# An adaLN transformer block with its gradients on one core: the preparation rewritten, and V, later Q, norms and modulation rows made inside the first attention chunk

## The chip, the cores and the metric

The kernel runs on one core of a Trainium2 chip. The metric is the device time of one execution in microseconds, from the first to the last instruction. Times of the kernel before are those of seven runs, and one more execution was taken with the hardware profiler. The core's engines are called PE (TensorE, matmuls; PEld is its weight load), DVE (VectorE), ACT (ScalarE), POOL (GpSimd) and SP (SyncE, which here only issues DMAs).

## What is computed

One transformer block with adaptive layer norm, and the gradients of all its parameters for a given output gradient. Sequence 2048, width 512, 32 heads of 16, hidden width 1792, all in bf16:

```
mod = (silu(c) @ w_mod).reshape(1, 6, 1, 512)        # sa, ca, ga, sb, cb, gb
h = layernorm(x) * (1 + ca) + sa
q, k, v = heads(h @ wqkv)
p = softmax(q @ k^T / 4)
x = x + ga * ((p @ v) @ wo)
h = layernorm(x) * (1 + cb) + sb
x = x + gb * (relu(h @ w1 + b1)**2 @ w2 + b2)
# results: x, and d/d(x, wqkv, wo, w1, b1, w2, b2, c, w_mod) of sum(x * grad_out)
```

## The kernel before

All work is on tiles of 128 partitions. The 2048 tokens are 16 tiles `t`, in four chunks of four tiles. There are four stages.

*Preparation* (L145 to L294, in pools of its own that are given back at its end). Loads, then for each chunk `g`: `layernorm(g)` takes statistics (bn_stats and bn_aggr on DVE), the reciprocal root by four Newton steps on DVE (`rsqrt_cols`), normalises on ACT, multiplies by `ca` and adds `sa` on DVE (rows spread over partitions, from `mod_rows(1)` and `mod_rows(0)`), and turns the result with DMA transposes into `h1T`. `qkv(g)` makes K, Q and V by tokens, twelve matmuls a tile, copies them out of PSUM, and turns K and Q with DMA transposes into `qkT`; all goes to DRAM (`qkT_st`, `v_st`, `k_st`, `q_st`), V also into `vaug` in SBUF, with a column of ones per head. `norms(g)` squares `qkT`, sums over each head with a selecting matmul, takes the greatest norm of the keys (`kmx`) and the root of those of the queries (`qn`). At the end `m_st` gets, for each head and query, minus the product of the two: the bound that is taken off the scores by an added row in `qt_sb`. Then come the modulation rows 2 to 5, their columns (`pcol`) and `b1col`. In preparation a scheduler orders the engines' work.

*Attention forward* (from L901). From here the written order is the order on each engine. A unit `u` is a chunk of 512 queries, a group of four heads and a tile of 128 keys: 4 x 8 x 16 = 512 units. `fscore(u)` makes four score matmuls of 32 rows into two PSUM pairs (`psST`, three buffers) and two Exp on ACT, each 128x1024, into `ET` (four buffers). `fpv(u - 2)` adds the products with `vaug` into `oacc`. Every 16 units `fload` loads the next group's K into `kts`, and Q and the row of `m_st` into `qts`, nine DMAs; `oacc` goes out through `ostage`, four DMAs to `rrows` and one DMA transpose to `O_un`. Beside this, each unit does at most one piece of other work through `step`: from the second chunk on, that is the dense half of the block and its gradients for the chunk before. All that other work shares one PSUM buffer, `pm`, from `mm()`. In the first chunk there is no such work; in its place SP runs `later_stage(u // 4)` and `turn_weights(u // 4)`, which turn V and the weights by DMA transposes for later stages. `later(lag, ...)` puts a call `lag` units further on; a DMA that `sp` issues waits in SP's queue, in order, for whatever it needs.

*The last chunk's dense half*, then *attention backward* (from L1457; 1300 us, half the span) and *the last products* follow. The change does not touch them, except that they read what the preparation stored: `k_st`, `q_st`, `vT_st`, `mean1`, `rstd1`, `rows_st`, `modcol`, `b1col`.

The unit loop before, as it bears on the change:

```
for u in range(NF + 2):
    unit[0] = u
    run_due()
    if u < NF:
        if funits[u][2] == 4 and u + TT < NF:
            fload(*funits[u + TT][0:2])
        fscore(u)
    if 2 <= u:
        fpv(u - 2)
    if u % 4 == 2 and u // 4 < 32:
        later_stage(u // 4)
    if u % 4 == 0 and u // 4 < 16:
        turn_weights(u // 4)
    if u < NF - 4:
        step(u)
```

Of the kernel before, what the change touches and what calls it, by code (L numbers as in the profile page):

```python
# [15 lines left out]
ALU = mybir.AluOpType  # L16
# [18 lines left out]
def kernel(  # L35
# [109 lines left out]
    with ExitStack() as ph:  # L145
        big = ph.enter_context(tc.tile_pool(name="prepB", bufs=1))
        wk = ph.enter_context(tc.tile_pool(name="prepW", bufs=2))
        psA = ph.enter_context(tc.tile_pool(name="psA", bufs=2, space=bass.MemoryType.PSUM))
        c_col = wk.tile([P, DC], BF, name="c_col", bufs=1)
        SP.dma_start(out=c_col[:], in_=c.rearrange("o (ic p) -> p (o ic)", p=P))  # L150
        x0_tok = big.tile([P, TT, D], BF, name="x0_tok")
        SP.dma_start(out=x0_tok[:, 0:4, :], in_=x_dram[:, 0:4, :])
        wmod_v = w_mod.rearrange("(ic p) j -> p ic j", p=P)
        wmod_nat = big.tile([P, DC, 6 * D], BF, name="wmod_nat")
        SP.dma_start(out=wmod_nat[:, :, 0:2 * D], in_=wmod_v[:, :, 0:2 * D])
        wqkv_nat = big.tile([P, DC, 3 * D], BF, name="wqkv_nat")
        SP.dma_start(out=wqkv_nat[:], in_=A_wqkv.rearrange("(ic p) j -> p ic j", p=P))
        for g in range(1, QC):
            SP.dma_start(out=x0_tok[:, 4 * g:4 * g + 4, :], in_=x_dram[:, 4 * g:4 * g + 4, :])
        SP.dma_start(out=wmod_nat[:, :, 2 * D:], in_=wmod_v[:, :, 2 * D:])  # L160
        b1bf = wk.tile([P, FC], BF, name="b1bf", bufs=1)
        SP.dma_start(out=b1bf[:], in_=B_b1.rearrange("(fc p) -> p fc", p=P))
        cbf = wk.tile([1, D], BF, name="cbf", bufs=1)
        SP.dma_start(out=cbf[:], in_=c[0:1, :])

        sig_col = wk.tile([P, DC], F32, name="sig_col", bufs=1)
        ACT.activation(sig_col[:], c_col[:], AF.Sigmoid)
        siluc_col = wk.tile([P, DC], BF, name="siluc_col", bufs=1)
        DVE.tensor_tensor(siluc_col[:], c_col[:], sig_col[:], ALU.mult)
        sbcT = big.tile([P, DC, P], BF, name="sbcT")  # L170
        DVE.tensor_copy(sbcT[:], siluc_col[:].unsqueeze(2).to_broadcast([P, DC, P]))
        crows = wk.tile([1, 3, D], F32, name="crows", bufs=1)
        ACT.activation(crows[:, 1, :], cbf[:], AF.Sigmoid)
        POOL.tensor_copy(crows[:, 0, :], cbf[:])
        POOL.tensor_tensor(crows[:, 2, :], crows[:, 0, :], crows[:, 1, :], ALU.mult)
        SP.dma_start(out=rows_st[6:9, :].unsqueeze(0), in_=crows[0:1, :, :])

        def mod_rows(j):
            pm = psA.tile([P, 512], F32, name="pm", tag="pm")
            for ic in range(DC):  # L180
                PE.matmul(pm[:], sbcT[:, ic, :], wmod_nat[:, ic, j * 512:(j + 1) * 512],
                          start=(ic == 0), stop=(ic == DC - 1))
            if j in (1, 4):
                DVE.tensor_scalar(modbc[:, j, :], pm[:], 1.0, None, ALU.add)
            else:
                ACT.activation(modbc[:, j, :], pm[:], AF.Identity)


        sel = big.tile([P, 4, H], BF, name="sel")
        POOL.memset(sel[:], 0.0)  # L190
        sel8 = wk.tile([P, 8], F32, name="sel8", bufs=1)
        DVE.tensor_reduce(sel8[:], identb.rearrange("p (i d) -> p i d", d=DH), AX.X, ALU.add)
        for b in range(4):
            POOL.tensor_copy(sel[:, b, 8 * b:8 * b + 8], sel8[:])
        POOL.memset(vaug[:, :, H, :], 1.0)
        POOL.memset(vaug[:, :, :, DH:DH + 1], 1.0)
        for i in range(2):
            POOL.memset(kts[i][:], 1.0)
            POOL.memset(qts[i][:], 0.0)

        h1T = big.tile([P, TT, DC, P], BF, name="h1T")
        qkT = big.tile([P, 8, n], BF, name="qkT")
        qn = big.tile([H, n], F32, name="qn")
        kmx = wk.tile([H, QC], F32, name="kmx", bufs=1)

        def layernorm(g):
            mv4 = wk.tile([P, 4, 2], F32, name="mv4p", tag="mv4p")
            for ti in range(4):
                st6 = wk.tile([P, 6], F32, name="st6p", tag="st6p")
                DVE.bn_stats(st6[:], x0_tok[:, 4 * g + ti, :])  # L210
                DVE.bn_aggr(mv4[:, ti, :], st6[:])
            gs = slice(4 * g, 4 * g + 4)
            rsqrt_cols(wk, rstd1[:, gs], mv4[:, :, 1], 4)
            DVE.tensor_copy(mean1[:, gs], mv4[:, :, 0])
            nb4 = wk.tile([P, 4], F32, name="nb4p", tag="nb4p")
            DVE.scalar_tensor_tensor(out=nb4[:], in0=mv4[:, :, 0], scalar=-1.0, in1=rstd1[:, gs], op0=ALU.mult, op1=ALU.mult)
            h1_g = wk.tile([P, 4, D], BF, name="h1_g", tag="h1_g")
            for ti in range(4):
                t = 4 * g + ti
                xn1 = wk.tile([P, D], BF, name="xn1", tag="xn1")  # L220
                ACT.activation(xn1[:], x0_tok[:, t, :], AF.Identity, bias=nb4[:, ti:ti + 1], scale=rstd1[:, t:t + 1])
                DVE.tensor_tensor(h1_g[:, ti, :], xn1[:], ca1_bc, ALU.mult)
                DVE.tensor_tensor(h1_g[:, ti, :], h1_g[:, ti, :], sa_bc, ALU.add)
                if ti % 2 == 1:
                    SP.dma_start(out=h1T[:, t - 1:t + 1].rearrange("p t i q -> p (t i) q"),
                                 in_=h1_g[:, ti - 1:ti + 1, :].rearrange("p t d -> p (t d)"), transpose=True)

        def qkv(g):
            qkv_g = wk.tile([P, 4, 3 * D], BF, name="qkv_g", tag="qkv_g")
            for ti in range(4):  # L230
                t = 4 * g + ti
                for which in (1, 0, 2):
                    pq = psA.tile([P, D], F32, name="pqkv", tag="pqkv", bufs=3)
                    for ic in range(DC):
                        PE.matmul(pq[:], h1T[:, t, ic, :], wqkv_nat[:, ic, which * D:(which + 1) * D],
                                  start=(ic == 0), stop=(ic == DC - 1))
                    dst = qkv_g[:, ti, which * D:(which + 1) * D]
                    if which == 0:
                        DVE.tensor_copy(dst, pq[:])
                    else:  # L240
                        ACT.activation(dst, pq[:], AF.Identity)
                SP.dma_start(out=qkT[:, :, t * P:(t + 1) * P], in_=qkv_g[:, ti, 0:2 * D], transpose=True)
# [27 lines left out]
        for g in range(QC):  # L270
            if g + 1 < QC:
                layernorm(g + 1)
# [1507 lines left out]
```

## Time and profile before

| what | us |
|---|---|
| median of 7 runs | 2637.76 (2627.47 to 2644.49) |
| the profiled execution | 2638.39 |
| its span, first to last instruction | 2636.6 |
| first score matmul (L705) / first Exp (L707) | 104.2 / 106.2 |
| dense half of the last chunk | about 1108 to 1220 |
| attention backward | about 1220 to 2520 |

The mean granted clock of TensorE was 0.883 of full speed over the span. The page gives busy time of each engine, the span in 40 equal slices, and the costliest groups of instructions, each with what ended the idle time before it. The chain of waits follows the work that ended last back to what released it. A busy share is an average over stages with different limits, so it is read by stages.

### The profile page before, as it was taken

How to read it: one execution, taken by the hardware profiler on the slowest of the kernel's cores; microseconds unless marked ns; L12 is line 12 of the kernel's file. 1: busy time of each engine (PE TensorE's matmuls, PEld its weight loads, DVE VectorE, ACT ScalarE, POOL GpSimd, SP SyncE). 2: the span in 40 equal slices, each digit the busy share in tenths (PEclk: the TensorE clock that was granted, in tenths of full speed). 3: DMA queues.
4: the chain of work that ended last, by engine and by line, in shares of the span. 5: the costliest groups of instructions: out<-in, count | busy, mean ns of one | idle time of the engine just before them, and what ended most of it. 6: DMA issues, size and time to landing. Idle time of an engine off the chain costs nothing.

```text
span 2636.6 us, 48844 instructions
## 1 busy us (share of the span) xinstructions
PE 2376.2 (90%) x18110; PEld 747.9 (28%) x18183; DVE 1748.5 (66%) x2234; ACT 2321.3 (88%) x3594; POOL 362.1 (14%) x369
## 2 busy tenths in 40 slices
PE   6699989988988889899999999999999999999999
PEld 2211112322322232352222222222222222222243
DVE  7101134434443544568999999998999998989962
ACT  4599999998999899855999999999999999999952
POOL 2100010211242223201110101101011010110100
PEclk8655559986999799998999999998999999999999
DMA  8853366335855775798999999999999999999982
GB/s 241 197 149 123 99 154 139 83 109 157 134 98 100 155 135 118 173 257 190 198 200 199 203 197 202 195 199 195 193 198 195 194 198 195 195 193 205 193 244 82
DMA packets 1254800, 453.74 MB, mean 172 GB/s; under 512 B 1130127, under 2 KB 1225363, under 8 KB 1254306
## 3 DMA queue, kind: packets, MB, share of 16 engines
q1 hardware_dynamic: 1226642, 415.77, 80.0%
q0 software_dynamic: 10944, 16.78, 4.5%
q10 hardware_dynamic: 16976, 18.07, 2.5%
q8 instruction: 143, 2.34, 0.4%
q14 instruction: 95, 0.78, 0.1%
HBM read 97.08 MB, written 73.95 MB: 65 GB/s over the span
## 4 chain that ended last, share of the span: by engine, by line
PE 43%; ACT 37%; issue 6%; DVE 5%; DMA 3%; SPq 1%; ACTq 0%; POOL 0%; DVEq 0%; POOLq 0%
ACT E_u L1346 20%; ACT ET L707 13%; PE dqacc L1418 6%; PE psS_A L1340 4%; PE psST L705 4%; PE accVK L1391 3%; ACT dsT L1489 3%; PE psS_C L1340 2%; PE pm L380 2%; PE psS_B L1340 2%; PE oacc L721 2%; PE pm L545 2%; PE accVK L1400 2%; PE pdh L1604 2%; PE pwq L1638 2%
## 5 line engine op out<-in xcount | busy, mean ns | idle before, releaser
L1360 DVE TENSOR_TENSOR dS_u<-psD_u,E_u 128x1024 bf16<-128x1024 f32 x1024 | 1186.4, 1215 | 106.5 <-PE psS_B L1340 55.1
L707 ACT ACTIVATE ET<-psST 128x1024 bf16<-128x1024 f32 x1024 | 945.0, 1296 | 43.7 <-PE psST L705 43.2
L1346 ACT ACTIVATE E_u<-psS_A 128x512 bf16<-128x512 f32 x768 | 509.6, 664 | 24.0 <-PE psD_u L1358 8.4
L1346 ACT ACTIVATE E_u<-psS_B 128x512 bf16<-128x512 f32 x768 | 504.8, 657 | 6.2 <-PE ptT L1381 1.2
L705 PE MATMUL psST<-qt_sb,kt_sb 32*128 32x512 bf16 x2048 | 412.8, 468 | 62.8 <-ACT ET L707 27.3
L1358 PE MATMUL psD_u<-iv,ido 32*128 32x512 bf16 x2048 | 425.7, 401 | 1.9 <-DVE dS_u L1360 1.7
L1346 ACT ACTIVATE E_u<-psS_C 128x512 bf16<-128x512 f32 x512 | 335.1, 654 | 1.5 <-PE accVK L1400 0.8
L1340 PE MATMUL psS_B<-ik,iq 32*128 32x512 bf16 x768 | 308.3, 401 | 11.8 <-ACT E_u L1346 4.4
L1340 PE MATMUL psS_A<-ik,iq 32*128 32x512 bf16 x768 | 306.7, 399 | 13.0 <-ACT E_u L1346 2.0
L721 PE MATMUL oacc<-ET,vaug 128*32 128x512 bf16 x2048 | 248.9, 476 | 5.9 <-DVE ostage L725 5.9
L1391 PE MATMUL accVK<-dS_u,qz 128*32 128x512 bf16 x2048 | 226.3, 412 | 0.5 <-DVE dS_u L1360 0.4
L1340 PE MATMUL psS_C<-ik,iq 32*128 32x512 bf16 x512 | 195.4, 382 | 32.9 <-ACT dsT L1489 28.8
L1340 PEld LDWEIGHTS <-iq 32*128 32x128 bf16 x2048 | 129.3, 92 | 309.0 <-issue 293.5
L1400 PE MATMUL accVK<-E_u,dOs_tok 128*16 128x512 bf16 x2048 | 208.3, 397 | 0.0
L705 PEld LDWEIGHTS <-kt_sb 32*128 32x128 bf16 x2048 | 90.2, 94 | 399.9 <-issue 388.7
L1436 POOL TENSOR_TENSOR dQacc<-dQacc,dqtmp 128x512 f32<-128x512 f32 x64 | 81.3, 1270 | 873.6 <-ACT dqtmp L1431 873.6
L1418 PE MATMUL dqacc<-dsT,KS_tok 128*32 128x512 bf16 x2048 | 180.7, 462 | 12.9 <-DMA dsT<-dS_u 3.5
L725 DVE COPY ostage<-oacc 128x512 f32<-128x512 f32 x32 | 22.0, 688 | 229.8 <-PE oacc L721 182.1
L1489 ACT ACTIVATE dsT<-ptT 128x1024 bf16<-128x1024 bf16 x128 | 148.5, 1160 | 3.3 <-PE ptT L1381 3.0
L398 DVE COPY part<-pm 128x512 f32<-128x512 f32 (+2 forms) x103 | 63.4, 616 | 132.5 <-PE pm L380 124.8
L1358 PEld LDWEIGHTS <-ido 32*128 32x128 bf16 x2048 | 107.3, 92 | 108.4 <-issue 103.9
L1391 PEld LDWEIGHTS <-qz 128*32 128x32 bf16 x2048 | 60.8, 98 | 241.0 <-issue 228.3
(342 smaller groups left out, 2255.8 us busy)
## 6 DMA issues: line engine op xcount, KB each, us to landing
p_st<-part POOLq DMA_DIRECT2D x36, 256.0 KB, 5.6
kt_sb<-qkT_st SPq DMA_DIRECT2D x128, 64.0 KB
wA<-in_B_w_dram SPq DMA_DIRECT2D x28, 256.0 KB
dsT<-dS_u SPq DMA_TRANSPOSE x448
wB<-w1T_st SPq DMA_DIRECT2D x21, 256.0 KB
wA<-w2T_st SPq DMA_DIRECT2D x21, 256.0 KB
wB<-in_B_w_dram SPq DMA_DIRECT2D x21, 256.0 KB
p_st<-part POOLq DMA_DIRECT2D x25, 192.0 KB, 4.1
```

The costliest lines, as they stand in the source:

```text
L705: PE.matmul(ps[:, hi, :], kt_sb[r:r + 32, kt * P:(kt + 1) * P], qt_sb[r:r + 32, :], start=True, stop=True, tile_position=(r, 0))
L707: ACT.activation(ET[:, 2 * pair:2 * pair + 2, :], ps[:], AF.Exp, scale=SCALE)
L721: PE.matmul(oacc[32 * hq:32 * hq + 32, :], lhsT, ET[:, hq, :], start=(kt == 0), stop=(kt == TT - 1), tile_position=(0, 32 * hq), skip_grou ...
L1340: PE.matmul(psS[:], st["q"][r:r + 32, qt * P:(qt + 1) * P], st["k"][r:r + 32, kc * 512:kc * 512 + 512], start=True, stop=True, tile_positi ...
L1346: ACT.activation(bst[u][0][:, hq, :], sst.pop((u, hq))[:], AF.Exp, scale=SCALE)
L1358: PE.matmul(psD[:, hi, :], st["do"][r:r + 32, qt * P:(qt + 1) * P], st["v"][r:r + 32, kc * 512:kc * 512 + 512], start=True, stop=True, til ...
L1360: DVE.tensor_tensor(dS_u[:, 2 * pair:2 * pair + 2, :], psD[:], E_u[:, 2 * pair:2 * pair + 2, :], ALU.mult)
L1391: PE.matmul(cur["vk"][32 * hq:32 * hq + 32, :], hst[hg]["qz"][:, qt, hq, :], bst[u][1][:, hq, :], start=(qt == 0), stop=False, tile_positi ...
L1400: PE.matmul(acc[32 * hq:32 * hq + DH, :], dOs_tok[:, qt, (hg * 4 + hq) * DH:(hg * 4 + hq + 1) * DH], E_u[:, hq, :], start=False, stop=(qt ...
L1418: PE.matmul(acc[32 * hq:32 * hq + 32, :], KS_tok[:, kc * 4 + kt, h * DH:h * DH + 32], tT[:, :, hq * 4 + kt, :], start=(kt == 0), stop=(kt ...
L1436: POOL.tensor_tensor(dst2, dst, tmp[:], ALU.add)
L1489: ACT.activation(dst, pt[:], AF.Identity)
```

## The change

The preparation leaves its own pools and becomes `prep()`, written out in order, in the pools of the forward stage.

- LN: statistics on DVE as before; the root on ACT and the reciprocal on DVE; POOL normalises; PE turns the tiles; ACT applies `1 + ca` and `sa` as columns while it copies out of PSUM. `mod_cols_of` makes these columns first, by 32 one-column matmuls.
- K is made turned, by heads on the partitions, with the weights as the stationary side: no DMA transpose. It goes to `kts[0]` straight from SBUF and to `qkT_st`. Norms of K follow. Of Q only the first chunk is made, the same way, with its norms; its row goes to `qts[0]` straight from SBUF.
- V: two tiles before the first unit, 14 as tasks.
- `tasks`, one taken per unit from `u = 0` on: 14 tiles of V (two DVE copies each), `b1` turned by PE, then for each later chunk four products of Q and seven tasks for its norms (the root by integer start and two Newton steps on DVE, 32x512), then rows 0 to 2, three loads of w_mod, three empty, columns 3 and 4, rows 3 to 5: 61 in all.
- K and Q by tokens (`k_st`, `q_st`) are made by `tokens(i)`, eight times between units 49 and 91: four DMA transposes from `qkT_st` each, for Q also a POOL copy.
- `later_stage` runs in another order (V is turned at units 42 to 54), `turn_weights` at units 56 to 116 instead of 0 to 60, and `fload(0, 0)` goes.

The core of the diff (all that is removed of the preparation is in the listing above):

```diff
+        def stats1(g):
+            gs = slice(4 * g, 4 * g + 4)
+            for ti in range(4):
+                st6 = wk.tile([P, 6], F32, name="st6p", tag="st6")
+                DVE.bn_stats(st6[:], xcs[g][:, ti, :])
+                DVE.bn_aggr(mv[:, 4 * g + ti, :], st6[:])
+            DVE.tensor_scalar(sd[:, gs], mv[:, gs, 1], EPS, None, ALU.add)
+            POOL.tensor_copy(mean1[:, gs], mv[:, gs, 0])
+            ACT.activation(sd[:, gs], sd[:, gs], AF.Sqrt)
+            DVE.reciprocal(rstd1[:, gs], sd[:, gs])
+        def normed1(g):
...
+            for ti in range(4):
+                t = 4 * g + ti
+                POOL.tensor_scalar(xn[:, ti, :], xcs[g][:, ti, :], mean1[:, t:t + 1], rstd1[:, t:t + 1], ALU.subtract, ALU.mult)
+            for pair in range(2):
+                pt = psp["p"].tile([P, 2, DC, P], BF, name="ptP", tag="pt", bufs=2)
+                for k in range(2):
+                    for ic in range(DC):
+                        PE.transpose(pt[:, k, ic, :], xn[:, 2 * pair + k, ic * P:(ic + 1) * P], identb[:])
+                for ic in range(DC):
+                    ACT.activation(h1T[:, 2 * pair:2 * pair + 2, ic, :], pt[:, :, ic, :], AF.Identity,
+                                   bias=modcol[:, 0, ic:ic + 1], scale=modcol[:, 1, ic:ic + 1])
+        def turned_proj(acc, which, g, hb):
+            for ic in range(DC):
+                PE.matmul(acc, wqkv[:, ic, which * D + hb * P:which * D + (hb + 1) * P], h1Ts[g][:, :, ic, :],
+                          start=(ic == 0), stop=(ic == DC - 1))
+        def keys(g):
+            KTs[g] = KT = ework.tile([P, 4, 512], BF, name="KT", tag="ET")
+            for hb in range(4):
+                pk = psp["p"].tile([P, 512], F32, name="pk", tag="pk", bufs=4)
+                turned_proj(pk[:], 1, g, hb)
+                ACT.activation(KT[:, hb, :], pk[:], AF.Identity)
+                if hb == 0:
+                    for h in range(4):
+                        sp(kts[0][32 * h:32 * h + DH, chunk_cols(g)], KT[DH * h:DH * h + DH, 0, :])
+            sp(qkT_v[:, 1, :, chunk_cols(g)], KT[:])
+        def value_tile(t, acc):
+            for ic in range(DC):
+                PE.matmul(acc, h1Ts[t // 4][:, t % 4, ic, :], wqkv[:, ic, 2 * D:3 * D], start=(ic == 0), stop=(ic == DC - 1))
...
+            DVE.tensor_copy(vaug[:, t, 0:H, 0:DH], acc.rearrange("p (h d) -> p h d", d=DH))
+            DVE.tensor_copy(psp["v"][:, t % 4, :], acc)
+            if t % 4 == 3:
+                later(1, sp, v_st.rearrange("(t p) d -> p t d", p=P)[:, t - 3:t + 1, :], psp["v"][:])
+        def query_tile(g, hb, acc):
+            turned_proj(acc, 0, g, hb)
+            lo = 4 + 4 * (g % 2)
+            DVE.tensor_copy(sP[:, lo + hb, :], acc)
+            if hb == 3:
+                later(1, sp, qkT_v[:, 0, :, chunk_cols(g)], sP[:, lo:lo + 4, :])
+        def prep():
...
+            stats1(0)
+            mod_cols_of(psp["p"].tile([P, 8], F32, name="pcol", tag="pcol", bufs=1), 0, 2)
+            stats1(1)
+            normed1(0)
+            stats1(2)
+            normed1(1)
+            keys(0)
+            stats1(3)
+            POOL.tensor_copy(crows[:, 0, :], cbf)
+            POOL.tensor_tensor(crows[:, 2, :], crows[:, 0, :], crows[:, 1, :], ALU.mult)
+            normed1(2)
+            keys(1)
+            key_norms(0)
+            normed1(3)
...
+            keys(2)
+            key_norms(1)
+            for hb in range(4):
+                pq = psp["p"].tile([P, 512], F32, name="pk", tag="pk", bufs=4)
+                query_tile(0, hb, pq[:])
...
+            keys(3)
+            key_norms(2)
...
+            sp(qts[0].rearrange("(h c) n -> c h n", h=4)[DH], mrow[0:4, :])
+            sp(m_st[:, 0:512], mrow)
+            for t in range(2):
+                pv = psp["p"].tile([P, 512], F32, name="pk", tag="pk", bufs=4)
+                value_tile(t, pv[:])
+        def plan_tasks():
+            for t in range(2, TT):
+                tasks.append(lambda t=t: value_tile(t, mm()[:]))
...
+            for j in (0, 1, 2):
+                tasks.append(lambda j=j: mod_rows(j))
+            for j in (3, 4, 5):
+                tasks.append(lambda j=j: sp(wmod_slice(j), wmod_v[:, :, j * D:(j + 1) * D]))
+            tasks.extend([lambda: None] * 3)
+            tasks.append(lambda: mod_cols_of(mm(), 3, 2))
+            for j in (3, 4, 5):
+                tasks.append(lambda j=j: mod_rows(j))
+        def tokens(i):
+            g, which = i % 4, 1 - i // 4
+            tok = cb.tile([P, 4, D], BF, name="tokP", tag=("a_c", "xn2_c")[i % 2])
+            for ti in range(4):
+                t = 4 * g + ti
+                sp(tok[:, ti, :], qkT_st[which][:, t * P:(t + 1) * P], True)
...
+        stages = [*range(4, 14), *range(4), *range(14, 32)]
...
-                fload(0, 0)
+                fh[0, 0] = (qts[0], kts[0])
...
-                        later_stage(u // 4)
-                    if u % 4 == 0 and u // 4 < 16:
-                        turn_weights(u // 4)
+                        later_stage(stages[u // 4])
+                    if u % 4 == 0 and 14 <= u // 4 < 30:
+                        turn_weights(u // 4 - 14)
+                    if u % 6 == 1 and 8 <= u // 6 < 16:
+                        tokens(u // 6 - 8)
+                    if tasks:
+                        tasks.pop(0)()
```

## The prediction

> **What bounds the kernel now.** I read the page first, then the chain of waits for the first 140 us, then busy time by stretches, and last the single rows that price a step.
>
> ```profile
> span 2636.6 us, 48844 instructions
> ...
> PE   6699989988988889899999999999999999999999
> ...
> ACT  4599999998999899855999999999999999999952
> ...
> PEclk8655559986999799998999999998999999999999
> ```
>
> One digit is 66 us. ACT is at 8 or 9 from the third digit on, except around 1110-1220 us and at the end; in the first two digits it is not. So the start is a stage of its own. The chain of waits shows what ends it:
>
> ```profile
> 96.56 0.80 DVE mrows L283 x2
> ...
> 97.55 1.51 DMA m_st<-mrows
> ...
> 102.09 1.82 DMA qt_sb<-m_st
> 103.92 0.24 issue
> 104.16 0.65 PE psST L705 x4
> ...
> 104.92 1.28 ACT L707
> ...
> 106.21 6.53 ACT ET L707 x7
> ```
>
> The first Exp starts at 106.21 us; what stands before it are the norm rows of the last chunk, a round trip of them through DRAM, ten loads on SP and a table load. The third view is busy time by stretches; its columns are PE, PEld, DVE, ACT and POOL busy (instructions), granted clock, DMA share, GB/s:
>
> ```profile
> 48.00:72.00 24.00, 23.64 (x104) 10.04 (x105) 9.03 (x11) 11.10 (x18) 7.46 (x4) 0.98 1.06 247
> 104.00:355.00 251.00, 229.92 (x1084) 43.03 (x1084) 28.25 (x35) 250.07 (x274) 9.32 (x15) 0.50 0.48 130
> 400.00:404.00 4.00, 4.00 (x19) 0.88 (x17) 1.18 (x2) 2.74 (x3) 0.00 (x0) 0.50 0.16 57
> 404.00:408.00 4.00, 3.71 (x32) 1.23 (x32) 3.18 (x6) 3.46 (x4) 0.22 (x1) 0.98 0.00 0
> 412.00:416.00 4.00, 3.48 (x28) 1.26 (x25) 2.60 (x5) 4.00 (x5) 0.00 (x0) 1.00 0.34 76
> ```
>
> In preparation (first row) PE and DMA are both full. In the first attention chunk (second row) ACT is busy all the time and PE 92% at a granted clock of 0.50. A unit (four heads, 128 keys, two Exp) takes 1.83 us there: the timeline's Exp start every 0.915 us. The last three rows are the start of a dense burst in the second chunk: ACT loses 1.26 and 0.54 us while the clock is low, then nothing.
>
> **What the change takes from the start.** I build the new start from rows of the old one. The first four tiles of x are there at 5.1 us (first bn_stats). Four bn_stats and bn_aggr are 4 x (0.68 + 0.17) = 3.4 us: 8.6. The w_mod columns are there at 8.3 (first L181 matmul); 32 one-column matmuls took 1.0 us (L290): 9.4, two column copies: 9.8. Statistics of group 1 stand behind those copies on DVE: 13.2, and POOL's copy of the means behind them: 13.5, before the first normalised tile, as the built program's order shows. The loads do not hold this up: 5.5 MB stand on SP, and the four-microsecond stretches from 4 to 20 us moved 356 to 404 GB/s, so all of it is there by some 18 us, each piece before it is wanted. The old transfer of b1 by single elements, behind which SP stood 8.1 us at L164, goes.
>
> Now 16 normalisations of 128x512 on POOL, for which no row exists. These bound them:
>
> ```profile
> L963 POOL TENSOR_SCALAR qz<-iqs 128x1024 bf16<-128x1024 bf16 x7 | 19.4, 2773 | 0.0
> L454 POOL TENSOR_TENSOR gf_c<-g_c,modbc 128x2048 bf16<-128x2048 bf16 x3 | 12.5, 4161 | 82.3 <-DMA g_c<-in_grad_out_dram 45.5 <-issue 36.9
> L816 POOL COPY tmpT<-tmpT 128x512 bf16<-128x512 bf16 x4 | 2.5, 613 | 21.1 <-DMA tmpT<-in_A_wqkv_dram 21.1
> ```
>
> A copy costs 0.61 us, a product of 512 columns 4.16 / 4 = 1.04, the same operation 2.77 / 2 = 1.39 beside a full DVE. I take 1.2, nearest to the last; ends 0.61 and 1.39. With the crows pair (0.60 + 1.26) and means, POOL ends at 13.5 + 16 x 1.2 + 2.1 = 35. Transposes, the activations that shift and scale (1.93 us for four, L1043: 3.9 a group), keys of groups 0 and 1 and their norms lie under this, and so do the five stores of each key group on SP (0.45 each); if POOL were instant they would be the path instead. Behind it on PE: a transposed pair 0.72 (L1039), then keys 2, queries 0, keys 3: 48 matmuls at 0.24 (L235 warm: 35 in 8.36 us) = 11.5, and one norm group of four, 1.0: 48. From there the chain is reduce, two squarings of 128x2048 (half of L257's 2.34 each), norm matmuls, reduce, root, row: 1.0 + 0.7 + 1.2 + 1.2 + 1.0 + 0.7 + 1.0 = 6.8, and 2.1 from issue to psST as at 102.09 above: 57; scores 0.7, no table load behind them: 58. A PE that is half cold there adds 2: **first Exp at 60**, 46 earlier. Ends: 53 with POOL at 0.61 (PE then follows), 74 with POOL at 1.39 (+3) and the whole tail at clock 0.50 (+11).
>
> **What comes back in the first chunk.** 61 tasks, one per unit. V: 14 tiles of four matmuls, two DVE copies each, and one PSUM buffer for all. How that buffer is passed on is seen in the timeline at the same kind of work:
>
> ```profile
> 373.46 1.04 PE L494 MATMUL pm<-wo_nat,OT 128*128 128x512 bf16 x4
> 375.63 0.68 DVE L495 CAST a_c<-pm 128x512 bf16<-128x512 f32 x1
> 376.36 1.02 PE L494 MATMUL pm<-wo_nat,OT 128*128 128x512 bf16 x4 [0.20 <-DVE a_c L495]
> ```
>
> PE goes on 0.05 us after the copy. So a V unit takes 1.02 + two copies 1.35 + 0.1 = 2.47 us, and scores of the next unit but one are queued behind the waiting matmul: 14 x (2.47 - 1.83) = 9 us (ends 0, if Exp never ran dry, and 14 x 1.85 = 26, cold). Queries (one copy, 1.02 + 0.69 + 0.1 = 1.81) fit once the clock is up. Between them lie seven units of norm work on DVE alone, about 0.5 to 0.7 us each, hidden by the Exp, which DVE has no part in. POOL's four copies of Q by tokens (1.92 each, L250) only move; the V copies it loses (1.95 each, L248) go to DVE, where they are priced above. In the norm units the clock falls (383.4 us in the timeline: 0.50 again 3.4 us after the last wo matmul), so four bursts start cold: groups 2 and 3 of the queries, rows 0-2, rows 3-5. Each costs what the rows at 400-408 lost, 1.8: 7 us (ends 0 and 16; cold throughout, a task of four costs 4 x 0.427 + 1.97 - 1.83 = 1.85).
>
> Rows 3-5 need w_mod again, three loads of 512 KB at units 51-53. SP is held by the m row of unit 48; behind it stand a V transpose 2.6, four token transposes 5.2 (w1T: 5.16 for four), row stores and output transpose 3.8, nine loads 4.4, three stores and a load 1.9: 18 us, ten units, plus 2 to land. The columns are wanted at unit 57, so PE waits some two units, and Exp behind it: 4 us (0 to 8). The 32 token transposes (42 us of SP) also push the loads of kt and qt. Between two of the row stores there are 32, 38 and 33 us of SP work where 29.3 pass, so these loads slip from on time to 16 us late by unit 100; with 27.5 us from row store to need and 10 for the loads they have 17: 0, at worst 8. Removed DMA (24 transposes of the preparation) costs nothing, since preparation is gone as a whole.
>
> **Sum.** -46 + 9 + 7 + 4 = -26. The profiled execution took 2638.4 us (span 2636.6 and 1.8 around it), 0.6 above the median of the runs: **2612 us**. After the first chunk nothing differs.
>
> **A rule against the trace.** The clock row above says 0.50 for 251 us in which PE is busy 92%. The Trainium skill ("TensorE: Matmul & The Clock Gate", Part 1) says that some 3.4 us of a busy PE release the full clock; here 32-row matmuls did not. By that rule the chunk would be warm all along and the 7 us would go: 2605. The same page (Part 4) says that transposes do not count as busy for the clock, which speaks against turning the LN on PE; by that the 64 transposes and the keys between them stay cold, 64 x 0.09 = 6 us more by L1039's row: 2618. No row here isolates it.
>
> **The rivals.** (1) The work in the chunk is free: at 412-416 us dense work costs ACT nothing. Then all 46 stay: 2592. Against it: the one PSUM buffer, and the cold row at 400. (2) The clock does not rise: each task is 4 matmuls in 16 units' worth of thin ones, and the 0.50 holds. Place: units 0-60; price: 14 + 12 + 6 full tasks and three norm groups, 35 x 1.85 = 65; 2638 - 46 + 65 = 2657, slower; it decides once more than 25 tasks run cold. For it: 0.50 at 92% busy. Against it: at 371-383 us four tasks, 2.9 us apart, kept the clock at 1.00. (3) The start is not much shorter: POOL at 1.39, a cold tail, Exp at 74, and 30 us come back: 2636, no change. That the code does not do what it says is excluded by the built order: the first Exp stands behind two V tiles only, the rest inside the chunk.
>
> **Chances.** Forecast 0.62, (1) 0.14, (2) 0.13, (3) 0.11. A measurement of this kernel can tell 0.3% (8 us) from no change. Faster takes the forecast and (1), 0.76; same is (3), with a little of the edge of the others, 0.11; slower 0.13. The range, 2592 to 2636, reaches from (1) to (3) and leaves out (2); it takes in Exp at 53 to 74 and 5 to 36 us given back.
>
> **What would show it.** First Exp near 60 us; the first 16 units in 36 to 42 us instead of 29.3; granted clock at 1.00 for most of the first 15 units, then up and down; ACT waiting for psST behind `pm`, and near unit 57 PE waiting for a DMA of wmod_nat; chunks two to four as before. First Exp after 75 us, or a first chunk over 280 us, would prove the sum wrong.

## The result, and the profile after

The changed kernel takes 2657.75 us (median of 23 runs, 2645.0 to 2669.8) against 2637.6 us for the kernel before (58 runs): a ratio of 1.0077, 95% interval 1.0065 to 1.0090, so 20 us slower. The forecast was 2612, faster; it was wrong in sign and outside its range. The profiled execution of the changed kernel took 2650.4 us (span 2648.6), 7 us under the median. All line numbers below are the changed kernel's; in it the Exp of the forward pass is L555 (L707 before) and the scores' matmul L553 (L705).

The page of the changed kernel, the rows that answer to those shown of before (one digit is 66 us, in tenths):

```profile
span 2648.6 us, 49041 instructions
...
PE   5779769988998888899999999999999999999999
...
ACT  4889779999999999955999999999999999999942
...
PEclk9875558998998799998999999899999999999999
```

ACT's first digits rose from 4 5 9 9 to 4 8 8 9: attention begins earlier. But digits five and six fell from 9 9 to 7 7, where there was no hole before. (The first digits of PEclk overstate the clock, as the next table's rows do; see below it.) The same in busy time by stretches (columns as before: PE, PEld, DVE, ACT, POOL, granted clock, DMA share, GB/s):

```profile
0.00:24.00 24.00, 3.79 (x50) 2.58 (x51) 13.84 (x39) 7.56 (x15) 15.44 (x24) 1.00 0.68 219
24.00:48.00 24.00, 14.45 (x80) 6.76 (x78) 6.49 (x14) 14.29 (x31) 23.91 (x14) 1.00 0.14 46
48.00:72.00 24.00, 19.37 (x75) 7.58 (x76) 11.00 (x16) 8.87 (x16) 3.05 (x3) 0.86 0.17 58
72.00:108.00 36.00, 25.11 (x178) 8.94 (x181) 18.40 (x30) 29.46 (x31) 3.50 (x6) 1.00 0.36 119
108.00:192.00 84.00, 70.33 (x405) 18.28 (x404) 39.02 (x60) 77.32 (x85) 3.08 (x5) 0.75 0.52 134
192.00:240.00 48.00, 39.25 (x231) 9.18 (x228) 7.03 (x12) 42.34 (x47) 0.73 (x1) 0.57 0.69 170
240.00:388.00 148.00, 106.82 (x516) 20.47 (x512) 24.42 (x30) 117.47 (x129) 14.27 (x8) 0.50 0.64 171
```

From 24 to 48 us POOL is busy 23.91 of 24 and no other engine is above 15: POOL is the path of the new start. From 240 to 388 us no engine is busy all the time (ACT 117 of 148), so something outside PE, DVE, ACT and POOL's own work sets the pace; before, ACT was busy all of the same stretch:

```profile
222.00:370.00 148.00, 137.13 (x655) 26.05 (x651) 29.64 (x37) 148.00 (x163) 6.85 (x5) 0.50 0.40 111
```

One column misleads. The profile holds no record of the clock before 34.8 us, and the rows count time without a record as 1.00. The timeline shows what the clock was (start, duration, in brackets the idle time before):

```profile
29.98 0.61 PE L767 MATMUL ptP<-identb,xnP 128*128 128x128 bf16 x4 [1.45 <-POOL xnP L762]
30.38 5.80 PE L774 MATMUL pk<-h1T,wqkv_nat 128*128 128x512 bf16 x16
...
38.17 0.40 PE L767 MATMUL ptP<-identb,xnP 128*128 128x128 bf16 x4 [1.55 <-POOL xnP L762]
...
40.46 3.62 PE L774 MATMUL pk<-h1T,wqkv_nat 128*128 128x512 bf16 x16
...
48.90 0.61 PE L767 MATMUL ptP<-identb,xnP 128*128 128x128 bf16 x4 [2.11 <-POOL xnP L762]
```

Four transposes took 0.61 us up to 30 us, 0.40 while the clock is recorded at 1.00 (34.8 to 48.4 us), and 0.61 again where it is recorded at 0.50 (48.4 to 51.9); sixteen matmuls of K took 5.80 and then 3.62. So up to 34.8 us the clock was low.

The first Exp stands at 72.94 us (106.21 before): 33.3 us are gained. Each further row of this table is the time from the first Exp of 16 units to the first Exp of the next 16, taken from the two traces (us):

| units from | 0 | 16 | 32 | 48 | 64 | 80 | 96 | 112 | 128 | 144 |
|---|---|---|---|---|---|---|---|---|---|---|
| before | 28.9 | 29.0 | 29.3 | 29.3 | 29.6 | 29.1 | 29.3 | 29.3 | 29.6 | 34.8 |
| after | 36.2 | 33.3 | 31.2 | 37.0 | 28.9 | 36.5 | 37.4 | 36.9 | 37.9 | 33.8 |

The first four groups give back 21.0 us, the four from 80 to 144 give back 31.3, the two others 1.7 the other way: 50.6 in all. Unit 160 begins at 421.9 us instead of 404.5, 17.3 later. From there to unit 400 the groups of the two kernels are alike. (The two profiled executions end 12.0 us apart, since the changed kernel's makes up 5 us behind unit 160; the medians are 20.1 apart, and executions of the changed kernel spread over 25 us.)

What the late groups wait for: the waits of PE from 239 to 389 us (us in total, times, longest) and of ACT:

```profile
PE psST L553 <- DMA qt_sb<-m_st: 24.4, 3, 8.7
PE pm L645 <- DMA rrows<-ostage: 9.0, 1, 9.0
```

```profile
ACT ET L555 <- PE psST L553: 30.5, 4, 8.6
```

Four waits of PE, one per group, and ACT behind each: the loss is there. The timeline at the one before unit 112 (start, duration, and in brackets the idle time before with what ended it):

```profile
310.70 0.56 SPq L138 DMA_DIRECT2D qt_sb<-m_st  x1
311.37 0.37 SPq L173 DMA_DIRECT2D h_st<-tmpT  x1
...
312.53 0.71 PE L553 MATMUL psST<-qt_sb,kt_sb 32*128 32x512 bf16 x4 [8.71 <-DMA qt_sb<-m_st]
...
313.26 3.77 ACT L555 ACTIVATE ET<-psST 128x1024 bf16<-128x1024 f32 x4 [7.91 <-PE psST L553]
```

The nine loads for unit 112 are asked for at unit 100, whose first Exp stood at 283.2 us. The last of them is issued at 310.7, when PE has been dry for 7 us (312.53 - 8.71 = 303.8). Why so late is in the chain of waits of 260 to 320 us (start, duration, what it was):

```profile
258.82 1.27 SPq L173
260.13 2.21 SPq L173
262.38 2.58 DMA tokP<-qkT_st
...
265.11 1.90 POOL qhg L183
267.03 0.38 SPq L173
267.45 1.88 SPq L173
269.43 0.52 SPq L138
...
273.22 0.55 SPq L138
273.82 1.43 SPq L173
275.36 1.20 SPq L173
```

In this stretch the chain does not rest on an Exp or a matmul: 65% of it are SP's own instructions (52.2% L173, with transposes of 1.25 us and more, and 12.8% L138, the loads standing behind them). Most of the rest is a load of x and DVE's work on it, beside which SP goes on issuing with hardly a pause. SP sets the pace.

### The profile page after: what moved, and what is told of

Read it like the earlier page. It is cut to its first block, busy times and chain, and to the rows that moved or that the text cites. A ratio compares the mean times of both kernels' runs of the same rounds, so it can differ in the third digit from the quotient of the medians.

```text
span 2648.6 us, 49041 instructions
## 1 busy us (share of the span) xinstructions
PE 2340.6 (88%) x18205; PEld 748.5 (28%) x18280; DVE 1777.3 (67%) x2218; ACT 2316.0 (87%) x3593; POOL 387.9 (15%) x383
## 4 chain that ended last, share of the span: by engine, by line
PE 43%; ACT 32%; DVE 7%; issue 6%; SPq 6%; DMA 4%; POOL 1%; ACTq 0%; DVEq 0%; another core or an unknown queue 0%; POOLq 0%
ACT E_u L1468 21%; ACT ET L555 7%; PE dqacc L1540 6%; SPq L173 4%; PE psS_A L1462 4%; PE psST L553 4%; ACT dsT L1611 3%; PE accVK L1513 3%; PE psS_C L1462 2%; PE psS_B L1462 2%; PE oacc L569 2%; PE pm L228 2%; PE accVK L1522 2%; PE pm L393 2%; PE pdh L1726 2%
## 5 line engine op out<-in xcount | busy, mean ns | idle before, releaser
L555 ACT ACTIVATE ET<-psST 128x1024 bf16<-128x1024 f32 x1024 | 948.1, 1151 | 90.7 <-PE psST L553 90.1
L1468 ACT ACTIVATE E_u<-psS_A 128x512 bf16<-128x512 f32 x768 | 505.9, 659 | 22.5 <-PE psD_u L1480 7.4
L553 PE MATMUL psST<-qt_sb,kt_sb 32*128 32x512 bf16 x2048 | 373.9, 446 | 82.1 <-ACT ET L555 36.6
L569 PE MATMUL oacc<-ET,vaug 128*32 128x512 bf16 x2048 | 238.5, 456 | 5.0 <-DVE ostage L573 5.0
L553 PEld LDWEIGHTS <-kt_sb 32*128 32x128 bf16 x2048 | 87.4, 93 | 391.1 <-issue 350.9
L1503 PE MATMUL ptT<-identb,dS_u 128*128 128x128 bf16 x1024 | 80.1, 222 | 32.9 <-ACT dsT L1611 25.9
```

The lines of the kernel that those rows point to most:

```text
L553: PE.matmul(ps[:, hi, :], kt_sb[r:r + 32, kt * P:(kt + 1) * P], qt_sb[r:r + 32, :], start=True, stop=True, tile_position=(r, 0))
L555: ACT.activation(ET[:, 2 * pair:2 * pair + 2, :], ps[:], AF.Exp, scale=SCALE)
L569: PE.matmul(oacc[32 * hq:32 * hq + 32, :], lhsT, ET[:, hq, :], start=(kt == 0), stop=(kt == TT - 1), tile_position=(0, 32 * hq), skip_grou ...
L1468: ACT.activation(bst[u][0][:, hq, :], sst.pop((u, hq))[:], AF.Exp, scale=SCALE)
```

## The experiments

Eleven kernels, each the changed kernel with the edits named. The times are medians with the ratio to the kernel before; "against the changed kernel" compares the distances to the kernel before (the changed kernel's is +20.1 us).

| run | us | ratio to before, 95% | against the changed kernel |
|---|---|---|---|
| loads on ACT's queue | 2706.9 | 1.0265 (1.0227 to 1.0302) | +48.5 |
| K tokens early | 2638.7 | 1.0006 (0.9991 to 1.0020) | -19.7 |
| normalisation on DVE | 2641.9 | 1.0010 (0.9991 to 1.0029) | -16.5 |
| one copy of V from PSUM | 2645.2 | 1.0026 (1.0010 to 1.0042) | -13.2 |
| all tokens early | 2653.6 | 1.0045 (1.0018 to 1.0071) | -4.4 |
| loads on POOL's queue | 2635.4 | 0.9992 (0.9975 to 1.0009) | -22.5 |
| rows and reload early | 2655.6 | 1.0068 (1.0041 to 1.0094) | -2.4 |
| four edits together | 2613.2 | 0.9904 (0.9872 to 0.9936) | -44.8 |
| K tokens in the dense work | 2641.7 | 1.0004 (0.9987 to 1.0020) | -17.2 |
| best | 2606.2 | 0.9869 (0.9841 to 0.9896) | -52.5 |
| one operation on POOL | 2648.6 | one run | |

### The loads of kt and qt on ACT's queue

```diff
-            load_rows(kt_sb, ...); load_rows(qt_sb, ...)
+            queue = ACT if unit[0] < 128 else SP
+            for to, fro in row_loads(...): queue.dma_start(out=to, in_=fro)
```

> Edit: the nine loads of kt and qt for a head group are issued on ACT's queue instead of SP's while the unit number is below 128; nothing else differs, and the DMA engines do the same work. Theory A (SP's in-order queue is behind, since 32 token transposes of 1.30 us and the weight transposes now stand in units 40 to 116, and the loads are queued behind them): the four slow groups of 16 units (80 to 144; 36.5 to 37.9 us each in the changed kernel) fall to 29 to 32.5, ACT losing at most 9 x 0.33 = 3 us a group for issuing; total 20 to 30 us below the changed kernel, 2628 to 2638. Rival 1 (the DMA engines or their bandwidth are what is behind, not the order of issue): the groups stay at 36 to 38 and the total is the changed kernel's or up to 10 us above. Rival 2 (the low clock: PE with dense tasks between is the bound): the groups stay at 36 to 38 also, but with PE busy and no wait for a DMA of kt or qt ahead of the scores.

It went the other way: 2706.9 us, and the first eight groups took 39 to 51 us. The timeline of this run shows why (ACTq are ACT's DMA issues):

```profile
245.23 9.10 ACTq L543 DMA_DIRECT2D kt_sb<-qkT_st  x3
258.75 6.41 ACTq L543 DMA_DIRECT2D qt_sb<-qkT_st  x4
265.51 0.50 ACTq L543 DMA_DIRECT2D qt_sb<-m_st  x1
```

The waits of ACT from 80 to 420 us:

```profile
ACT ET L557 <- DMA qt_sb<-qkT_st: 35.4, 4, 12.1
ACT ET L557 <- DMA tokP<-qkT_st: 34.7, 2, 21.7
```

Nine issues that take 4 to 5 us on SP in the changed kernel take 21, and between them the Exp stand still. In the trace the DMAs of SP's and of ACT's queue signal the same eight semaphores, some 180 DMAs of SP and 40 of ACT on each, and POOL's signal eight others. ACT waits 34.7 us for transposes of the tokens, which SP issues: its loads stood behind SP's DMAs all the same. The run says nothing of the DMA engines behind the queues.

### The K tokens early

```diff
+                    if u in (3, 9, 15, 21):
+                        tokens(u // 6)
-                    if u % 6 == 1 and 8 <= u // 6 < 16:
+                    if u % 6 == 1 and 12 <= u // 6 < 16:
```

> Edit: the four token tasks of K (each four DMA transposes of 1.30 us on SP and what follows) run at units 3, 9, 15 and 21 instead of 49 to 67; those of Q stay. Theory A (SP's queue is behind in units 50 to 144): some 21 us of SP work leave the late stretch, so that the loads of kt and qt come back in time for two to three of the four slow groups; these lose 15 to 30 us in sum, total 2628 to 2643; the first three groups grow by no more than 2 us, as SP has slack there. Rival (DMA engines or clock): the moved work is the same and the sum of the groups 80 to 144 falls by less than 5 us.

Groups 80 and 96 came back to 29.1 and 31.2 us; 112 and 128 stayed at 38.7 and 37.7. The four groups fell by 11.9 us together, short of the 15 that were expected; the total fell by 19.7 us, the first three groups grew by 1.0 (101.6 against 100.6). This is what the queue's order says. It does not yet exclude busy DMA engines, since the bytes of these transposes left the late stretch as well; the loads on POOL's queue, below, settle that.

### The normalisation on DVE

```diff
-                POOL.tensor_scalar(xn[:, ti, :], ..., ALU.subtract, ALU.mult)
+                DVE.tensor_scalar(xn[:, ti, :], ..., ALU.subtract, ALU.mult)
```

> Edit: the 16 normalisations of 128x512 run on DVE instead of POOL. In the changed kernel POOL takes 2.09 us for one, 33.4 us in all, and PE's transposes wait 22.6 us for them; on DVE the same shape took 0.41 us in the kernel before. Theory B (POOL is the path of the start, and the price of this row is what the forecast of the first Exp missed): the first Exp moves from 72.9 to 55 to 62 us, total 11 to 18 us below the changed kernel, 2640 to 2647. Rival (keys, norms and loads behind it set the start, as for POOL at 0.61): the first Exp stays above 68 and the total falls by less than 5.

The first Exp moved from 72.9 to 59.1 us and the total by 16.5. The row in the changed kernel and in this one:

```profile
L762 POOL TENSOR_SCALAR xnP<-xP,mean,rstd 128x512 bf16<-128x512 bf16 x16 | 33.4, 2092 | 0.0
```

```profile
L762 DVE TENSOR_SCALAR xnP<-xP,mean,rstd 128x512 bf16<-128x512 bf16 x16 | 5.7, 417 | 0.0
```

One instruction costs five times as much on POOL, and this price is what the forecast of the first Exp missed. The first Exp is not exact to a microsecond: in the six other runs whose preparation is that of the changed kernel, it stood between 70.1 and 73.2 us.

### One copy of V from PSUM

```diff
-            DVE.tensor_copy(psp["v"][:, t % 4, :], acc)
+            POOL.tensor_copy(psp["v"][:, t % 4, :]..., vaug[:, t, 0:H, 0:DH])
```

> Edit: the second copy of a V tile (for the store of V by tokens) is made by POOL from the first copy in SBUF, not by DVE from PSUM, so that DVE holds the one PSUM buffer for one copy of 0.68 us instead of two. Theory C (a V unit takes 2.40 us for 1.02 + two copies through one buffer): a V unit takes 1.8 to 1.9 us and the first 16 units 29 to 31 instead of 36.2; total 6 to 10 us below the changed kernel, 2648 to 2652. Rival (the units are slow since PE's dense matmuls stand between the thin ones of the scores, whatever the copies): the first group stays above 34 and the total within 3 us.

The first 16 units took 28.9 us, as in the kernel before: with one copy a V unit fits beside the Exp. The second and third took 32.6 and 32.0 (33.3 and 31.2 in the changed kernel); what they lose has little to do with V. The total fell by 13.2, more than the 6 to 10 expected; the first group explains 7.3 of it, and the rest was not followed up.

### All tokens early

```diff
-                    if u % 6 == 1 and 8 <= u // 6 < 16:
-                        tokens(u // 6 - 8)
+                    if u in TOK:                       # 3, 7, 11, 15, 19, 38, 41, 45
+                        tokens(TOK.index(u))
```

> Edit: all eight token tasks run early (K at units 3, 7, 11, 15; Q at 19, 38, 41, 45) instead of at 49 to 91. With the four K tasks alone moved, groups 80 and 96 came back to 29.1 and 31.2 us and groups 112 and 128 stayed at 38.7 and 37.7. Theory A (SP's queue is behind from unit 50 on, by what was moved into it): the other two come back as well, all four at 29 to 31, total 27 to 34 us below the changed kernel, 2624 to 2631. Rival (the last two groups are late for the transposes of w_mod that stand there in both kernels): they stay at 36 to 39 and the total is that of the run with K alone, 2636 to 2642.

The four groups came back as theory A said, the last not quite (29.1, 29.3, 29.3, 32.3), and yet the total fell by 4.4 only, where 27 to 34 were expected: the group of units 48 to 64 took 52.9 us. The waits of PE there, from 71 to 300 us:

```profile
PE pm L819 <- DMA wmod_nat<-in_w_mod_dram: 21.1, 2, 15.0
```

SP is full early now, so the three reloads of w_mod, asked for at units 51 to 53, come 15 us late. The work was not made less; it was pushed in front of another load. (The total rests on five executions, 2638.9 to 2654.9; in the profiled one unit 160 begins 13 us earlier than in the changed kernel.) The late stretch itself, by busy time as above:

```profile
226.00:345.00 119.00, 110.11 (x522) 20.62 (x520) 25.07 (x30) 119.00 (x132) 2.80 (x4) 0.50 0.58 147
```

ACT is busy 119.00 of 119 us at a clock of 0.50: the low clock is not what slows this stretch down in the changed kernel, where it is 0.50 too.

### The loads on POOL's queue

```diff
+            queue = POOL if unit[0] < 128 else SP
```

> Edit: the nine loads of kt and qt for a head group are issued on POOL's queue, which has completion semaphores of its own and is nearly empty in the first chunk, instead of SP's, while the unit number is below 128; the DMA engines do the same work. (On ACT's queue these loads shared SP's eight completion semaphores and stood behind SP's transposes, so that that run told nothing of the engines.) Theory A (order and issue on SP): groups 80, 96, 112 fall to 29 to 32 us; total 18 to 28 us below the changed kernel, 2630 to 2640. Rival (DMA engines or their bandwidth): the groups stay at 36 to 38, total 2650 or more.

Groups 80, 96 and 112 fell to 31.6, 31.3 and 28.9 us. So the DMA engines could deliver, with their share at 0.85 from 240 to 330 us (0.64 from 240 to 388 us in the changed kernel); what was late was the place behind SP's transposes. The total is 22.5 us below the changed kernel, as theory A said. But group 128 rose to 46.2. PE's waits from 330 to 400 us:

```profile
PE pm L647 <- DMA rrows<-ostage: 15.2, 1, 15.2
```

The row stores of the finished head groups still stand on SP. They hold up nothing until the chunk ends, when the dense work of the chunk needs the rows; then SP's backlog is paid at once.

### Rows 0 to 2 and the reload right after V

```diff
-            for j in (0, 1, 2): tasks.append(... mod_rows(j))
-            for j in (3, 4, 5): tasks.append(... reload j)
-            tasks.extend([lambda: None] * 3)
+            tasks[15:15] = [rows 0, 1, 2, reload 3, 4, 5]
```

> Edit: modulation rows 0 to 2 and the three reloads of w_mod stand right after V, before the query groups, some 30 units ahead of the columns that need the reload. Theory D (group 48 to 64 loses 7.6 us: some 4 for the reload that PE waits for, some 3.6 for two bursts that start at a granted clock of 0.50): that group falls from 37 to 30 to 33, the group of units 16 to 32 grows by at most 2; total 2 to 6 us below the changed kernel. Rival (the reload is hidden by the Exp, and the rows themselves are what costs): the group's loss moves to 16 to 32 unchanged, total within 2 us of the changed kernel.

Group 48 fell from 37.0 to 30.8 us, group 32 rose from 31.2 to 35.6 and group 16 fell from 33.3 to 31.3: the wait for the reload is gone (about 4 us), and the burst of dense work has moved. The total fell by 2.4 us, which this comparison (four executions, interval 1.0041 to 1.0094) cannot tell from no change.

### The four edits together

> Edit: the four edits together: tokens early, normalisation on DVE, the second V copy by POOL from SBUF, rows 0 to 2 and the reload right after V. If the four losses are independent and are the whole of what the forecast missed: first Exp at 57 to 61 us, the nine groups of units 0 to 144 at 29 to 33 each, total 2657.8 - 30 - 16 - 10 - 4 = 2598, range 2592 to 2608, 1.3 to 1.7% below the kernel before. Rival (what is taken out of one wait comes back in the next, since SP and ACT have little slack in this chunk): 2612 or more.

2613.2 us: faster than both kernels, but on the rival's side of what was expected (the interval, 2604 to 2621 us, reaches a little into the other). First Exp at 58.3, the late groups at 29.0 to 31.9; but groups 16 and 48 took 37.5 and 41.4. As with all tokens early, SP has little room from unit 0 to 64 (12 us of waits in 142), and now kt and qt are late there (PE waits 17.7 us in two waits for the loads).

### K tokens in the dense work of the finished chunks

```diff
             w2T = load_wA(w2T_st[:], 1)
             yield 3
+            tokens(c if c == 0 else c + 1)
...
+                if c == 0 and fc == 6:
+                    tokens(1)
```

> Edit: the four token tasks of K leave the first attention chunk; two run inside the dense work of the first finished chunk, one each in the next two. Those of Q stay, and nothing else of the changed kernel differs. SP's rows: in the nine groups of the first chunk it issues 103 transposes in 165 us and 182 plain DMAs in 105 us, 271 us where nine undisturbed groups take 264. Theory A2 (SP's issue time over the whole chunk is the bound, not the place of a task in it): the issue falls to some 250 us, the sum of the nine groups from 315 us to 293 or less, no group but the first four over 32 except the last of the chunk, total 2626 to 2634, better than with K early (2639). Rival (place matters, not the sum): late groups remain as with K early, 2636 to 2642. Second rival (the later chunks have no room either): groups 144 to 400 grow by what the first chunk gains, 2645 or more.

Theory A2 fell. The chunk as a whole had less for SP to do, and the total was 2641.7, within the rival's 2636 to 2642: groups 112 and 128 stayed at 39.7 and 37.5 us, as with K early. The later chunks took the four tasks at no cost that shows (units 144 to 400 in 501.6 us; 499.2 in the changed kernel, 502.2 before). So it is not the sum over the chunk. What it is shows when SP's instructions are added up by stretch (each counted to the start of the next one; times in us, transposes and plain DMAs as issued, waits apart):

| units 64 to 144 | transposes | plain DMAs | issue together | waits | length |
|---|---|---|---|---|---|
| before | 31, 50.4 | 86, 45.5 | 95.9 | 49.3 | 146.9 |
| changed kernel | 74, 113.8 | 94, 52.8 | 166.6 | 10.9 | 177.5 |
| K tokens early | 64, 100.7 | 92, 53.2 | 153.9 | 11.5 | 165.6 |
| K tokens in the dense work | 64, 104.0 | 91, 53.0 | 157.0 | 9.5 | 166.6 |
| loads on POOL's queue | 73, 115.8 | 58, 36.1 | 151.9 | 14.1 | 166.9 |
| all tokens early | 48, 81.3 | 87, 49.7 | 131.0 | 18.0 | 148.9 |
| best | 56, 92.0 | 89, 51.5 | 143.5 | 7.8 | 152.2 |

Issue and waits add up to the length by construction, so the sum proves nothing; the issue column does the work. In the four rows of 166 to 178 us it is 152 to 167, above the 147 us that five groups of Exp take, and SP has hardly a wait left in which to catch up. In the three others it is below 147, and they take 147 to 152. Both ways of taking out the K tokens leave some 155 us of issue, and both end at 166 us. (What is called a wait and what issue can be set otherwise; by another rule the issue is 3 to 10 us less in each row; it is then 147 to 164 in the four and 92 to 137 in the three.)

### The best version

The edits of the four together, but K's tokens in the dense work and Q's at units 9, 38, 61 and 73, so that SP is overfull in neither half.

> Edit: K tokens as in the run beside it, Q tokens at units 9, 38, 61 and 73, and with them the normalisation on DVE, the second V copy by POOL from SBUF, and rows 0 to 2 with the reload right after V. The four edits with all tokens early gave 2613, and left two groups late by 8 and 12 us and two by some 3 to 5. Theory A2: the late groups go, the nine groups of the first chunk sum to 275 us or less, total 2588 to 2600, 1.4 to 1.9% below the kernel before. Rival (the loss moves once more, to a wait behind SP that is not one of issue time): 2606 or more.

2606.2 us, 1.3% below the kernel before and 1.9% below the changed one. First Exp at 57.5 us; the nine groups sum to 279.9 us (315.1 in the changed kernel). The expected 275 and 2600 were missed: groups 16 and 32 still lose 3 and 6 us, and group 128 another 6, where PE waits once more for the rows at the chunk's end. That is the wait behind SP that the rival named; the interval, 2597 to 2611 us, does not part the two by time. The waits of PE from 58 to 360 us in this run:

```profile
PE psST L556 <- ACT ET L558: 11.8, 31, 0.5
PE pm L648 <- DMA rrows<-ostage: 5.9, 1, 5.9
PE pm L794 <- DVE sqP L792: 4.2, 3, 1.4
```

No wait for kt or qt is left among PE's.

### One operation on POOL

```diff
-                POOL.tensor_scalar(..., mean1[...], rstd1[...], ALU.subtract, ALU.mult)
+                POOL.tensor_scalar(..., mean1[...], None, ALU.subtract)
```

> Edit: POOL's normalisation only subtracts the mean; the product with the reciprocal deviation is left out, so that the instruction has one operation with a per-partition operand instead of two. In the changed kernel each of the 16 took 2.06 us whether DVE was busy beside it or idle. Theory B2 (POOL pays for each operation of the instruction): 1.0 to 1.2 us each, first Exp at 57 to 63. Rival (the price is that of the per-partition operand or of the form, not of the second operation): 1.8 to 2.1 each, first Exp above 68.

```profile
L762 POOL TENSOR_SCALAR xnP<-xP,mean 128x512 bf16<-128x512 bf16 x16 | 26.7, 1678 | 0.0
```

1.68 us on the mean (1.55 for fourteen of the sixteen, 2.06 for most before): neither theory. The second operation costs 0.41 us, or 0.51 by the undisturbed ones; the rest comes with one operation already, and what makes it up (the operand per partition, or what any such instruction costs there) stays open. The first Exp was at 65.0 us, 8.0 earlier; 16 x 0.41 = 6.6 of it is POOL's path. The total is a single execution and isn't used.

## Why the prediction was wrong

**The start, 46 us gained: 33.3.** The step that failed is the price of one row: "I take 1.2, nearest to the last; ends 0.61 and 1.39". It was 2.09, above the upper end, which came from an instruction with one operation and no operand per partition; with the second operation left out it was still 1.68, so the operation is 0.41 of the difference and the other part stays open. 16 x (2.09 - 1.2) = 14.2 us. Everything round it held: the first normalised tile began at 13.3 us (13.5 in the forecast), and from POOL's end (48.8) to the first Exp it took 24.1 us (35 to 60, so 25). With the row on DVE the first Exp came at 59.1. The Trainium skill ("GPSIMD Engine Reference", section 3.1) gives about 2.6 cycles for an element on this engine where DVE takes one, measured there for tensor_tensor with two input tensors; by an estimate from that figure and the clock of 1.2 GHz in the same page's section 1, 512 elements are 1.1 us. The instruction here has one input tensor, and its measurement, 2.09 with two operations and 1.68 with one, is well above that estimate, and decides.

**V, 9 us: 7.2, right.** The unit was to take 2.47 us through one buffer and two copies. The timeline of the changed kernel:

```profile
75.21 1.02 PE L800 MATMUL pm<-wqkv_nat,h1T 128*128 128x512 bf16 x4 [0.80 <-DVE vP L804]
...
77.61 1.02 PE L800 MATMUL pm<-wqkv_nat,h1T 128*128 128x512 bf16 x4 [0.72 <-DVE vP L804]
```

One unit every 2.40 us, PE waiting for the second copy in each, as worked out; the run with one copy removed the loss entirely.

**Cold bursts 7 us and the reload 4 us: 13.8 by the groups of 16 to 64, against 11.** The clock was 1.00 in V's stretch and fell to 0.50 and rose again four times from 120 to 209 us, as foreseen (0.75 and 0.57 on the mean in the next two stretches). Taken unit by unit, from the first Exp of one to that of the next less 1.83 us, the loss stands in three places. Units 26, 27, 37, 48, 49, 58 and 59, the first dense tasks behind each stretch of norms, lose 6.4 us while the clock is recorded at 0.50; the forecast had 7. Unit 57 loses 4.9 to the reload, where the forecast had 4. And units 19, 30 and 41, in which PE waits for DVE's squares of the queries, lose 3.0: this norm work was put at nothing, as "hidden by the Exp". The other units give 0.5 back. PE's waits from 72 to 240 us show the second and the third:

```profile
PE pm L819 <- DMA wmod_nat<-in_w_mod_dram: 4.4, 1, 4.4
...
PE pm L791 <- DVE sqP L789: 4.0, 3, 1.4
```

Moving the reload took its wait away, and the three groups fell from 101.4 to 97.7 us. That the low clock is the cause of the 6.4 rests on where they stand; no run isolates it. The price of 1.8 for a burst also took in 0.54 us from a row whose clock reads 0.98, not "while the clock is low".

**Loads late on SP, "0, at worst 8": 31.3 us.** This is the step that turned the sign, and it failed twice. First, the count was too small. Between row stores the forecast had 32, 38 and 33 us of SP work; the stores were issued at 182.8, 221.6, 263.7 and 302.7 us, so it was 38.8, 42.1 and 39.0, of which SP waited 6 us in all. The 54 transposes among it took 82 us, 1.5 each, where the forecast took 1.30 for one of a token task. That is 32 us late by unit 100 against the 16 of the forecast, and less the slack of 17 it is the 15 us that the groups of 80 and 96 lost. Second, the count was broken off at unit 100, "16 us late by unit 100", when 24 transposes of w_mod, there in both kernels, stood in units 106 to 126: the next distance between row stores was 37.2 us, and the group of 112 lost another 7.6. At the end of the chunk PE needs the last row stores themselves. Their issue began 16.6 us after the first Exp of unit 130, before the change 3.9, so 12.7 later; PE took them up 3.8 us after it instead of 8.2, a slack of 4.4, and the group of 128 lost the 8.3 that are left. Slack absorbs a lateness once; when it is used up, an in-order queue that gets more work than the time allows takes its excess from every group until the work ends. Before, SP waited 49 us from unit 64 to 144; 43 further transposes took 38 of that and 31 us more.

So: -33.3 + 7.2 + 13.8 + 31.3, and -1.7 for the two other groups, is +17.3 at unit 160, against +20.1 by the medians. With these two terms put right, the forecast's own sum reads 2638.4 - 46 + 14.2 + 9 + 7 + 4 + 31.3 = 2657.9; that it meets the median so closely is luck, as the 3.0 us of the norms are not in it and the two profiled executions end 12 us apart.

**The rivals.** (1), free work in the chunk, and (3), POOL at 1.39, did not happen, though (3) had the right engine. (2) came closest in time, 2657, and was wrong in its mechanism: the clock did rise with the dense tasks, and with all tokens early ACT was busy without a gap at a clock of 0.50. On the rule against the trace: up to 30 us PE's work was transposes behind POOL, and they ran at the low clock, 0.61 us for four against 0.40 later; the clock rose at 34.8 us, 4.4 us after the first matmul of K. This agrees with the rule of the Trainium skill ("TensorE: Matmul & The Clock Gate", Part 4: transposes don't count as busy in the same way), but PE was also busy for only 0.61 of every 2.06 us, and no run here tells the two apart. The 6 us that the rule would have added did not reach the time, since PE stood waiting for POOL there (22.6 us up to the first Exp), and the tail behind POOL took 24.1 us where 25 were forecast.

## What to carry to other kernels

An issue queue is an engine: add up what it issues by stretch, waits included, and compare it with the time that the stretch has; a row of "late by so much" must be followed to the end of the work, not to where the slack seems enough. A load that is late is cured by taking work off its queue in that stretch; pushing the work ahead only makes the next load late, as two of the runs showed (the reload with all tokens early, kt and qt with the four edits together). And the price of an instruction on another engine is worth more care when that engine will be the path: a bound from a simpler instruction on it is a lower one.

## What was not expected of the hardware

- A DMA transpose of 128x512 held SP for 1.25 to 1.30 us when nothing was in its way, and all transposes of units 64 to 144 took 1.54 us on the mean with what they wait for (113.8 us for 74); a plain DMA 0.56 us (52.8 for 94).
- A subtraction and product with operands per partition, 128x512 in bf16, took 2.06 us on POOL both with DVE busy beside it (2.08 us with DVE busy for 2.02 of them) and with DVE idle (2.06), so work of DVE beside it is not the reason.
- DMAs issued from ACT's queue were held up by SP's, nine issues over 21 us; from POOL's queue they were not, nine in 4 to 9 us.
- With all tokens early the granted clock stayed at 0.50 for 119 us in which PE was busy 110, all of it in matmuls of 32 rows (scores) or 32 columns (products with V); in the changed kernel it was 1.00 while tasks of four dense matmuls, 1.02 us, came every 2.40 us. Where the profile has no record of the clock (up to 34.8 us), only the durations of like matmuls show it.
